# One PSUM pool of eight single banks, evictions by the bank, and a new list of jobs for all engines

## The chip, the cores and the metric

The kernel runs on one core of a Trainium2 chip. The metric is device time in microseconds (us). TensorE (PE) does the matrix products into PSUM, VectorE (DVE) and ScalarE (ACT) read PSUM and write SBUF, GpSimd (POOL) works from SBUF to SBUF, and SyncE (SP) issues the transfers. PSUM has eight banks; a bank holds 512 float32 values in each of 128 partitions.

## The reference

A retention layer (attention without softmax, with a decay by distance) feeds a gated MLP with spatial gating.

```python
# q, k, v: (8, 8, 576, 64) float32
scores = q @ k.T / sqrt(64)
Dmat   = where(i >= j, gamma[h] ** (i - j), 0)          # per head
x      = (scores * Dmat) @ v                            # heads side by side: (8, 576, 512)
h      = gelu_tanh(x @ w_in)                            # (8, 576, 1024)
u, v   = h[..., :512], h[..., 512:]
v_n    = (v - mean(v)) / sqrt(var(v) + 1e-6) * g_ln
v_s    = w_sg @ v_n + b_sg                              # over the sequence
out    = x + (u * v_s) @ w_out                          # (8, 576, 512) float32
```

## The kernel before, in words

The eight batches are taken as four pairs. A pair has 1152 rows, nine tiles (`m`) of 128 rows, and is cut into five blocks (`n`, table `RB`): four blocks of 256 rows and, in the middle, one of 128 rows that holds the end of the first batch and the start of the second. Block `b` is 5 times the pair plus `n`, so there are 20 blocks.

For each block:

- `a_load` fetches q, k and v (on SP). `a_prep` writes them to SBUF as bfloat16: q and v times powers of the decay, k as it is. POOL does nearly all of this; block 0 has its q on DVE and its k on ACT.
- `a_T` transposes q and k on PE, `a_Tev` copies the result out of PSUM (`qT`, `kT`). For blocks from 10 on, apart from the middle blocks, `a_TX` does it by DMA.
- `a_S(b, g)` makes the scores of chunks, `a_Sev` multiplies them by the causal mask into `ret`. `a_Z` makes the running state k.T @ v; `a_Zsum` and `a_Zev` add it up and turn it into bfloat16.
- `a_O` and `a_O2` make the output from `ret`, v, q and the state. `a_Oev` copies it to `xT`.
- `m_V` makes the gate half of x @ w_in, `m_Vg` is its gelu (ACT), `m_stats` the mean and variance (DVE), `m_rs` the reciprocal root (POOL), `m_norm` the normalization (ACT). `m_U` and `m_Ug` do the other half.

Once all tiles of a batch are normalized, `m_W` multiplies by `wT` (the transposed `w_sg`, made once by `build_wT` and `evac_wT`), `m_Wg` multiplies the gate into `uT` (DVE), `m_O` makes the output, `m_Oev` copies it out (ACT in the first pair, where PE adds x; DVE with `xr` in the others), and `m_store` stores it. At the start, `win_load`, `sg_load` and `wo_load` bring in the weights and cast them, on ACT with two casts on DVE (each job there is called `g`).

The order of all of this is written out by hand: every step is a job with a number, and `ORDER` lists the numbers. `emit` goes through the list and issues each job's instructions; each engine and the transfer queue of SP work in that order. In the list `f2w64` is a warm-up fill (matmuls of zeros), and `3@267` holds job 3 until PE is through with job 267.

PSUM is cut into two pools: `psP` with two slots of two banks for the transposed q and k, the scores and the attention outputs (all called `pp`), and `psD` with four single banks for the rest. Each pool hands out its slots in turn, in the order in which the jobs ask. The two banks of a `pp` slot are read by one instruction where DVE reads them (`a_Tev` L422, `a_Sev` L471), and by two, one for each bank, in `a_Oev` (L597).

Of the kernel before, what the change touches and what calls it, by code (L numbers as in the profile page):

```python
# [103 lines left out]
def kernel(  # L104
# [113 lines left out]
    def fill(spec):  # L218
# [3 lines left out]
        def f():  # L222
            scr = psD.tile([128, 512], F32, name="scr", tag="d")
            for _ in range(n):
                nc.tensor.matmul(scr[:, :w], warm[:, :128], warm[:, :w], start=True, stop=True, skip_group_check=True)
# [861 lines left out]
```

## Time and profile before

| | |
|---|---|
| time, median of 3 runs | 208.69 us (208.69 to 208.93) |
| span of the profiled execution, first to last instruction | 207.8 us |
| PE busy | 189.1 us, 91% |
| DVE busy | 146.6 us, 71% |
| ACT busy | 116.3 us, 56% |
| POOL busy | 118.3 us, 57% |
| moved by DMA | 50.45 MB, mean 243 GB/s |

The profile is of one execution. Its own time is not listed beside it; its span is 0.9 us below the median of the timed runs, which counts what lies ahead of the first and behind the last instruction too. Busy time of PE counts overlapping matmuls once, and a busy PE may still be at half its rate. In the groups of instructions, the number after "x" is the count, then come busy us and mean ns of one, then the engine's idle time before them and what ended it. In a row of the order in time come start, length, engine, line, and in square brackets the idle time before it.

### The profile page before, as it was taken

What the parts mean: (1) busy time and instruction counts of PE and PEld (TensorE: products, weight loads), DVE (VectorE), ACT (ScalarE), POOL (GpSimd) and SP (SyncE); (2) the same over time, 40 slices, a digit from 0 to 9 for tenths busy, and PEclk for the clock granted to TensorE, in tenths of its full rate; (3) what the DMA queues carried; (4) which work ended last, traced back from release to release, by engine and by line L of the source; (5) the groups of instructions that cost most, each with busy time, mean ns of one, the idle gap of its engine ahead of it and who ended that gap; (6) DMA issues with size and microseconds to landing.
All of it is one profiled execution on the core that took longest, in us unless ns stands there. A gap on an engine that the chain in (4) does not pass through costs nothing. (4 is left out here: it accounts for less than half of the span.)

```text
span 207.8 us, 7603 instructions
## 1 busy us (share of the span) xinstructions
PE 189.1 (91%) x3231; PEld 130.0 (63%) x3260; DVE 146.6 (71%) x287; ACT 116.3 (56%) x207; POOL 118.3 (57%) x169
## 2 busy tenths in 40 slices
PE   3277989999999979999999999999999999999992
PEld 3256467786667655666777676676675776556651
DVE  3767549897597669646968479669695648876672
ACT  5263398864659436689477565745827580536300
POOL 8747348864858799884659628760558813022000
PEclk9999999999999999999999999999999999999998
DMA  5999989989958999599999989999899999659765
GB/s 163 287 313 215 312 282 317 295 241 326 304 123 226 264 335 336 161 231 174 221 288 351 179 183 333 250 139 206 232 299 334 182 242 253 171 169 169 261 140 203
DMA packets 93844, 50.45 MB, mean 243 GB/s; under 512 B 44970, under 2 KB 87218, under 8 KB 93810
## 3 DMA queue, kind: packets, MB, share of 16 engines
q1 hardware_dynamic: 93792, 49.96, 93.8%
q8 instruction: 25, 0.41, 0.9%
q14 instruction: 9, 0.07, 0.1%
q10 hardware_dynamic: 18, 0.00, 0.0%
HBM read 32.79 MB, written 9.44 MB: 203 GB/s over the span
## 5 line engine op out<-in xcount | busy, mean ns | idle before, releaser
L471 DVE TENSOR_TENSOR ret<-pp,msk 128x1024 bf16<-128x1024 f32 x32 | 38.3, 1214 | 7.5 <-PE pp L458 7.4
L674 PE MATMUL wp<-wT,vn 128*128 128x288 bf16 x256 | 40.6, 286 | 0.0
L370 POOL TENSOR_TENSOR vb<-ld,gpow 128x1024 bf16<-128x1024 f32 (+1 forms) x20 | 34.5, 1731 | 10.2 <-PE pp L458 6.1
L608 PE MATMUL hv<-w_in,xT 128*128 128x512 bf16 x132 | 36.5, 393 | 1.9 <-ACT xT L597 1.0
L684 DVE TENSOR_TENSOR uT<-wp,uT 128x288 bf16<-128x288 f32 x64 | 27.6, 450 | 14.9 <-PE wp L674 10.3
L655 PE MATMUL hu<-xT,w_in 128*128 128x256 bf16 (+1 forms) x320 | 36.3, 262 | 0.0
L615 ACT ACTIVATE vg<-hv 128x512 f32<-128x512 f32 x36 | 21.2, 595 | 25.0 <-PE hv L608 20.7
L705 PE MATMUL op<-w_out,uT 128*128 128x512 bf16 (+1 forms) x131 | 33.5, 373 | 0.8 <-issue 0.2
L655 PEld LDWEIGHTS <-w_in 128*128 128x128 bf16 x320 | 28.1, 98 | 6.2
L623 DVE BATCH_NORM_STATS2 bst<-vg 128x6 f32<-128x512 f32 x36 | 24.6, 683 | 8.8 <-ACT vg L615 8.7
L597 ACT ACTIVATE xT<-pp 128x512 bf16<-128x512 f32 (+1 forms) x40 | 20.8, 549 | 17.2 <-PE pp L540 17.2
L370 POOL TENSOR_TENSOR qb<-ldq,gpow 128x1024 bf16<-128x1024 f32 x14 | 26.4, 1902 | 5.3 <-DMA ldq<-in_q_dram 5.3
L674 PEld LDWEIGHTS <-vn 128*128 128x128 bf16 x256 | 24.3, 98 | 8.2
L643 ACT ACTIVATE vn<-vg,mv 128x512 bf16<-128x512 f32 x32 | 25.2, 809 | 6.5 <-POOL mv L631 6.4
L628 POOL TENSOR_SCALAR mv<-mv 128x2 f32<-128x2 f32 (+1 forms) x20 | 4.5, 224 | 41.6 <-DVE mv L624 36.5
L665 ACT ACTIVATE uT<-hu 128x512 bf16<-128x512 f32 x36 | 20.7, 594 | 10.2 <-PE hu L655 10.1
L724 DVE TENSOR_TENSOR ob<-op,xr 128x512 f32<-128x512 f32 (+1 forms) x28 | 18.4, 669 | 5.8 <-PE op L705 5.5
L608 PEld LDWEIGHTS <-xT 128*128 128x128 bf16 x144 | 13.4, 100 | 14.2 <-ACT xT L597 1.6
L705 PEld LDWEIGHTS <-uT 128*128 128x128 bf16 x148 | 13.5, 98 | 11.4
L674 PE MATMUL wp<-wT,vmid 128*128 128x288 bf16 x64 | 18.2, 287 | 0.1
L360 POOL CAST kb<-ld 128x1024 bf16<-128x1024 f32 x14 | 14.5, 1037 | 4.8 <-DMA ld<-in_k_dram 4.8
L629 POOL TENSOR_TENSOR mv<-mv,mhalf 128x2 f32<-128x2 f32 (+1 forms) x20 | 14.1, 705 | 1.7
(100 smaller groups left out, 238.2 us busy)
## 6 DMA issues: line engine op xcount, KB each, us to landing
out_dram<-ob SPq DMA_DIRECT2D x35, 256.0 KB, 3.1
ld<-in_v_dram SPq DMA_DIRECT2D x16, 512.0 KB, 5.7
ld<-in_k_dram SPq DMA_DIRECT2D x16, 512.0 KB, 6.5
ldq<-in_q_dram SPq DMA_DIRECT2D x7, 1024.0 KB, 10.4
xT<-in_moe_w_sg_dram SPq DMA_DIRECT2D x2, 576.0 KB
ld<-in_q_dram SPq DMA_DIRECT2D x2, 512.0 KB, 5.2
xT<-in_moe_w_in_dram SPq DMA_DIRECT2D x1, 1024.0 KB
ld<-in_q_dram SPq DMA_DIRECT2D x8, 128.0 KB, 4.2
```

The source lines that it names most:

```text
L370: ve.tensor_tensor(dst, src, g.unsqueeze(len(src.shape) - 1).to_broadcast(list(src.shape)), op=Alu.mult)
L471: ins = nc.vector.tensor_tensor(ret[:].rearrange("p r (k t) -> p (r k) t", k=2), sc[:].rearrange("p r (k t) -> p (r k) t", k=2), (msk2 if ...
L597: nc.scalar.activation(dst, src, Act.Copy)
L608: ins = nc.tensor.matmul(hv[:], xTs[p][:, m, kk, :], w_in[:, kk, F2:], start=(kk == 0), stop=(kk == KK - 1))
L615: unfence(nc.scalar.activation(vgs[i][:], cur.pop(("hv", i))[:], Act.Gelu_apprx_tanh), ("V", i))
L623: nc.vector.bn_stats(bst[:], vgs[i][:])
L643: nc.scalar.activation(vn[:], vg[:], Act.Identity, scale=mv[:, s, 2:3], bias=mv[:, s, 3:4])
L655: ins = nc.tensor.matmul(hu[:, n, :], w_in[:, kk, 128 * c:128 * c + 128], xTs[p][:, m:m + w, kk, :], start=(kk == 0), stop=(kk == KK - 1), ...
L665: unfence(nc.scalar.activation(uTs[p][:, c0:c1, 128 * m:128 * m + 128 * w], cur.pop(("hu", i, half))[:], Act.Gelu_apprx_tanh), ("U", i, half))
L674: ins = nc.tensor.matmul(ps[:], vns[t0 + j][e][:, 128 * c:128 * c + 128], wT[e][j][:, half * HS:(half + 1) * HS], start=(j == 0), stop=(j ...
L684: ins = nc.vector.tensor_tensor(uTs[p][:, c, col:col + HS], cur.pop(("wp", b, c, half))[:], uTs[p][:, c, col:col + HS], op=Alu.mult)
L705: ins = nc.tensor.matmul(op[:], uTs[p][:, c, r], w_out[:, c, cs], start=(p >= XP and c == 0), stop=(c == KK - 1), skip_group_check=True)
```

## The change

- One pool `ps` of eight single banks takes the place of `psP` and `psD`. The tiles of two banks become two tiles of one bank each.
- `a_Tev` and `a_Sev` become two jobs each, one for each bank, so that there are 961 jobs in place of 913.
- A job may have an `alt`: another engine that can do it. In the list, `~` behind a number means that the job goes to that engine. A helper `copy` issues a copy on DVE, ACT or POOL; `m_norm` gets a DVE form (`tensor_scalar` with the scale and the bias), the casts of `w_out` too.
- Some dependencies become `after` or fall away, which matters only for whatever made the list, since the semaphores follow from the tiles.
- The list is new. It has one fill (`f4w192`, four products of 192 columns) in place of four (`f2w128`, `f2w64` twice, `f6w128`), and one hold (`876@857`) in place of eleven.

Jobs whose engine differs, by count:

| job | before | after |
|---|---|---|
| `a_Sev` | 36 DVE | 72 DVE (by the bank) |
| `a_Tev` | 12 DVE | 9 DVE, 15 ACT (by the bank) |
| `a_prep` | 58 POOL, 1 DVE, 1 ACT | 42 POOL, 11 DVE, 7 ACT |
| `m_norm` | 36 ACT | 19 ACT, 17 DVE |
| `a_Oev` | 40 ACT | 32 ACT, 8 DVE |
| `m_Oev` | 9 ACT, 28 DVE | 6 ACT, 31 DVE |
| `a_Zsum` | 32 DVE | 26 DVE, 6 ACT |
| `a_Zev` | 24 ACT | 19 ACT, 5 DVE |
| `evac_wT` | 10 DVE | 7 DVE, 3 ACT |
| weight casts `g` | 11 ACT, 2 DVE | 4 ACT, 9 DVE |

The diff, cut to its core (of the lists only their starts):

```diff
 ORDER = (
-    '0 2 103 73 105 1 f2w128 f2w64 7 17 6 75 76 8 77 78 108 109 104 267 22 269 72 3@267 106 107 268 270 12 13 195 81 '
...
+    '2 0 74 103~ 1 75 3 6 73 105~ 104 106 315 316~ 72 76 7 13 318 107~ 79 5~ 109~ 12 108~ 17 77 8 f4w192 4~ 207 210 '
+    '78 209 208 14 211 317 110 112 319~ 113 114~ 15 212 16 213 214 9 80 22~ 23 81 115 320 321 322 116 215 118 119 31 '
...
+            other, x = x[-1] == "~", x.rstrip("~")
...
-            j.fn()
+            j.fn(j.alt[0]) if other else j.fn()
...
-                xr=3, pp=2, d=4)
+                xr=3, d=8)
...
-    psP = ctx.enter_context(tc.tile_pool(name="psP", bufs=2, space=bass.MemoryType.PSUM))
-    psD = ctx.enter_context(tc.tile_pool(name="psD", bufs=4, space=bass.MemoryType.PSUM))
+    ps = ctx.enter_context(tc.tile_pool(name="ps", bufs=8, space=bass.MemoryType.PSUM))
+
+    def copy(eng, dst, src):
+        if eng == "ACT":
+            return nc.scalar.activation(dst, src, Act.Copy)
+        return (nc.vector if eng == "DVE" else nc.gpsimd).tensor_copy(dst, src)
...
+    def read(ins, what, n):
+        cur["left", what] = cur.get(("left", what), n) - 1
+        unfence(ins, what, cur["left", what] == 0)
...
-        tp = psP.tile([128, 2, 1024], BF, name="pp", tag="pp")
+        tp = [ps.tile([128, 1024], BF, name="tp", tag="d") for r in range(2)]
...
-    def a_Tev(b, t):
-        dst, w = new_T(b, t)
-        ins = nc.vector.tensor_copy(dst[:, :w].rearrange("p (c w) -> p c w", c=2), st.pop((b, "tp", t))[:, :, :w // 2])
-        unfence(ins, ("T", b, t))
+    def a_Tev(b, t, r, eng):
+        if ("Tw", b, t) not in cur:
+            cur["Tw", b, t] = new_T(b, t)
+        dst, w = cur["Tw", b, t]
+        ins = copy(eng, dst[:, r * w // 2:(r + 1) * w // 2], st.pop((b, "tp", t, r))[:, :w // 2])
+        read(ins, ("T", b, t), 2)
...
-        sc = psP.tile([128, 2, 512], F32, name="pp", tag="pp")
+        sc = [ps.tile([128, 512], F32, name="sc", tag="d") for r in range(2)]
...
-    def a_Sev(b, g):
+    def a_Sev(b, g, r):
...
+            m = (msk2 if joint(b) else msk4)[:].rearrange("p a b t -> p (a b t)").unsqueeze(1).to_broadcast([128, 2, 256])
+            ins = nc.vector.tensor_tensor(ret.rearrange("p (k t) -> p k t", k=2), sc[:].rearrange("p (k t) -> p k t", k=2), m, op=Alu.mult)
...
-        ot = psP.tile([128, 2, 512], F32, name="pp", tag="pp")
+        ot = [ps.tile([128, 512], F32, name="ot", tag="d") for c in range(2)]
...
-        nc.scalar.activation(dst, src, Act.Copy)
+        copy(eng, dst, src)
...
-    def m_norm(i):
+    def m_norm(i, eng="ACT"):
+        def norm(dst, src, scale, bias):
+            if eng == "ACT":
+                nc.scalar.activation(dst, src, Act.Identity, scale=scale, bias=bias)
+            else:
+                nc.vector.tensor_scalar(dst, src, scale, bias, op0=Alu.mult, op1=Alu.add)
```

More of the change, by code (lines that the diff above doesn't have):

```diff
@@ L62, with __init__ @@
 class Job:
-    def __init__(self, eng, dur, due, fn, deps=(), new=None, uses=(), mode=None, nbytes=0, run=0, what="", behind=None, since=0.0, lag=0.0, ins=0, port=False, parts=1):
+    def __init__(self, eng, dur, due, fn, deps=(), new=None, uses=(), mode=None, nbytes=0, run=0, what="", behind=None, since=0.0, lag=0.0, ins=0, port=False, parts=1, alt=None, after=()):
+        self.alt, self.after = alt, [d for d in after if d is not None]
         self.what, self.behind, self.since, self.lag, self.ins, self.port, self.parts = what, behind, since, lag, ins, port, parts
@@ L222, in f @@
         def f():
-            scr = psD.tile([128, 512], F32, name="scr", tag="d")
+            scr = ps.tile([128, 512], F32, name="scr", tag="d")
             for _ in range(n):
@@ L284, in sg_load @@
         ld.append(add("SP", 450.0, 0.0, f_last, new=b1, nbytes=64 * S * 4, run=2304))
-        return ld, [add("ACT", 677.0, 0.0, lambda j=j: g(j), deps=[ld[j // 2]], uses=[bA if j < 4 else b1]) for j in range(SB)]
+        return ld, [add("ACT", 677.0, 0.0, lambda eng="ACT", j=j: g(j, eng), deps=[ld[j // 2]], uses=[bA if j < 4 else b1], alt=("DVE", 420.0)) for j in range(SB)]
     def wo_load():
@@ L484, in a_Z @@
         ns, cs = RB[b % NBK][0], ZC[b % NBK]
-        z = {c: psD.tile([128, 256], F32, name="zp", tag="d") for c in cs}
+        z = {c: ps.tile([128, 256], F32, name="zp", tag="d") for c in cs}
         for c in cs:
@@ L694, in m_O @@
         cs = slice(0, DM) if hf is None else slice(hf * DM // 2, (hf + 1) * DM // 2)
-        op = psD.tile([128, cs.stop - cs.start], F32, name="op", tag="d")
+        op = ps.tile([128, cs.stop - cs.start], F32, name="op", tag="d")
         cur["op", i, hf] = op
@@ L875 @@
         kfst = not jn and half_of(b) == 0
-        jk = add(eng, 855.0 * h + 183, t0 - 4000.0, lambda b=b, eng=eng: a_prep(b, "k", None, eng),
-                 deps=[J["ld", b, "k"]] + (jqs if jn and b else [J["k", b - 1]] if not jn and not kfst else []), behind=jqs[0] if jn else None,
+        jk = add(eng, 855.0 * h + 183, t0 - 4000.0, lambda eng=eng, b=b: a_prep(b, "k", None, eng), alt=("POOL" if eng == "ACT" else "ACT", 855.0 * h + 183),
+                 deps=[J["ld", b, "k"]], after=jqs if jn else [J["k", b - 1]] if not kfst else [],
                  new=B_qkb["k", U_] if kfst else None,
                  uses=[B_ld[b, "k"]] + ([B_qkb["q", U_]] if jn else [] if kfst else [B_qkb["k", U_]]))
-        jvv = add("POOL", 1715.0 * h + 190, t0 - 2000.0, lambda b=b: a_prep(b, "v"), deps=[J["ld", b, "v"]],
+        jvv = add("POOL", 1715.0 * h + 190, t0 - 2000.0, lambda eng="POOL", b=b: a_prep(b, "v", None, eng), alt=("DVE", 126.0 + 1100.0 * h), deps=[J["ld", b, "v"]],
                   new=B_vb[b], uses=[B_ld[b, "v"]])
@@ L929 @@
                 B_run[b, c] = Buf("run")
-            J["run", b, c] = add("DVE", 400.0, due, lambda b=b, c=c: a_Zsum(b, c), deps=[jz] + ([J[("run",) + was]] if was else []),
+            J["run", b, c] = add("DVE", 400.0, due, lambda eng="DVE", b=b, c=c: a_Zsum(b, c, eng), alt=("ACT", 400.0) if fst else None, deps=[jz] + ([J[("run",) + was]] if was else []),
                                      new=B_zb[b, c] if fin else B_run[b, c], uses=[zpb[c]] + ([B_run[was]] if was else []))
@@ L950 @@
             fst = n == 0 and c == 0
-            J["x", b, c] = add("ACT", 600.0 if ns == 2 else 385.0, jO.due + 700.0 + 100 * c, lambda b=b, c=c: a_Oev(b, c),
-                               deps=[jO] + ([J["x", p * NBK, 0]] if not fst else []), new=B_x if fst else None,
-                               uses=[otb] + ([] if fst else [B_x]))
+            J["x", b, c] = add("ACT", 600.0 if ns == 2 else 385.0, jO.due + 700.0 + 100 * c, lambda eng="ACT", b=b, c=c: a_Oev(b, c, eng), alt=("DVE", 640.0 if ns == 2 else 375.0),
+                               deps=[jO], after=[J["x", p * NBK, 0]] if not fst else [], new=B_x if fst else None,
+                               uses=[otb[c]] + ([] if fst else [B_x]))
         B_mv = Buf("mv")
@@ L1044 @@
                                        uses=[B_x, B_u], mode="F", ins=17)
-                            jOe = add("ACT", 597.0, due + 700.0, lambda a=a: m_Oev(*a), deps=[jOut], uses=[db, obb])
+                            jOe = add("ACT", 597.0, due + 700.0, lambda eng="ACT", a=a: m_Oev(*a, eng), alt=("DVE", 640.0), deps=[jOut], uses=[db, obb])
                         else:
```

136 lines of the change are left out of this document (68 added, 68 removed), and 65 rows, old and new, of the table ORDER.

## The prediction, made before the changed kernel was run

> **What bounds the kernel now.** I read the page first: the shares of the engines, the chain that ended last, then the busy time by stages, then PE's order of work in the first 30 us.
>
> ```profile
> span 207.8 us, 7603 instructions
> PE 189.1 (91%) x3231; PEld 130.0 (63%) x3260; DVE 146.6 (71%) x287; ACT 116.3 (56%) x207; POOL 118.3 (57%) x169
> PE 34%; issue 1%; DVE 0%; DVEq 0%
> 0.00:30.00 30.00, 19.40 (x379) 13.79 (x382) 17.90 (x48) 15.31 (x26) 18.25 (x43) 1.00 0.95 256
> 30.00:203.00 173.00, 168.88 (x2848) 115.71 (x2874) 127.44 (x237) 101.03 (x182) 100.07 (x127) 1.00 0.96 242
> 203.00:207.80 4.80, 0.78 (x8) 0.45 (x5) 1.30 (x3) 0.00 (x0) 0.00 (x0) 0.87 0.55 203
> 40.00:50.00 10.00, 9.38 (x259) 7.35 (x257) 8.66 (x14) 6.67 (x12) 5.39 (x5) 1.00 0.94 292
> 70.00:80.00 10.00, 8.41 (x210) 6.17 (x210) 6.02 (x14) 4.07 (x8) 8.99 (x9) 1.00 1.14 313
> 76.77 0.64 PE L407 MATMUL pp<-ident,qb 64*128 64x64 bf16 x32 [1.54 <-POOL qb L370]
> ```
>
> The reader is to see three stages (the columns of a stage are its length, then PE, PEld, DVE, ACT and POOL busy, the granted clock, the DMA share and GB/s). From 30 to 203 us PE is the bound: busy 168.88 of 173.00, 4.1 idle. The chain that ended last is PE work back to 130 us. Of those 4.1, 1.59 lie in 70 to 80 us and 0.62 in 40 to 50. The one long stop there is 1.54 us before a transposition, waiting for POOL's q preparation while POOL is busy 8.99 of 10. DVE is busy 127.44 of 173.00, or 74%. The end, 4.8 us, is the last copies and stores and has the same jobs in both lists. PE's matmuls are the same in both kernels except warm-up fills. So the change can only gain in the first 30 us and in the 4.1 us, and can only lose by new idle time of PE.
>
> The span is 207.8 and the median of the runs 208.69, so 0.9 us lie outside the span. I take differences from the span and apply them to 208.69.
>
> **The change, term by term. The first 30 us.**
>
> ```profile
> 8.63 1.06 ACT L358 ACTIVATE qb<-ld 128x1024 bf16<-128x1024 f32 x1 [3.20 <-DMA ld<-in_k_dram]
> 10.31 1.03 PE L407 MATMUL pp<-ident,qb 64*128 64x64 bf16 x32
> 12.67 0.64 PE L458 MATMUL pp<-qT 64*64 64x128 bf16 x16 [1.32 <-DVE qT L422]
> 16.96 0.32 PE L540 MATMUL pp<-ret,vb 64*64 64x128 bf16 x2
> 10.45 0.51 SPq L248 DMA_DIRECT2D xT<-in_moe_w_in_dram  x1
> 19.11 0.69 DVE L255 CAST w_in<-xT 128x1024 bf16<-128x1024 f32 x1 [0.81 <-DMA xT<-in_moe_w_in_dram]
> 20.71 0.61 PE L608 MATMUL hv<-w_in,xT 128*128 128x512 bf16 x1 [0.77 <-ACT xT L597]
> 23.64 1.89 PE L608 MATMUL hv<-w_in,xT 128*128 128x512 bf16 x4
> 32.69 1.89 PE L608 MATMUL hv<-w_in,xT 128*128 128x512 bf16 x8
> 27.77 1.60 PE L225 MATMUL scr<-warm 128*128 128x128 f32 x12
> 29.60 0.81 PE L608 MATMUL hv<-w_in,xT 128*128 128x512 bf16 x3 [0.23 <-ACT xT L597]
> GB/s 163 287 313 215 312 282 317 295 241 326 304 123 226 264 335 336 161 231 174 221 288 351 179 183 333 250 139 206 232 299 334 182 242 253 171 169 169 261 140 203
> L422 DVE COPY qT<-pp 128x1024 bf16<-128x1024 bf16 x4 | 2.7, 681 | 0.0
> L257 ACT ACTIVATE w_in<-xT 128x1024 bf16<-128x1024 f32 x1 | 1.1, 1057 | 4.3 <-DMA xT<-in_moe_w_in_dram 4.3
> L370 DVE TENSOR_TENSOR qb<-ld,gpow 128x1024 bf16<-128x1024 f32 x1 | 1.2, 1226 | 1.6 <-DMA ld<-in_q_dram 1.6
> ```
>
> Before: k of block 0 lands at 8.63, transposition 10.31, first scores 12.67, first O 16.96, first m_V 20.71; all attention of blocks 0 to 2 and both m_V of block 0 are through at 27.77. Then 12 fills, and real work goes on at 29.60.
>
> After, by hand from these rows. k is again the third large load: ACT prepares it by 9.7, transposition and Z until 11.3. ACT then has one Zsum (0.4) and both halves of the transposition (1057 ns each, the row of a copy as long), so S(0,0) starts near 13.9, 1.2 us later than now. The load of w_in's gate half loses its hold (`3@267`) and goes fourth. With q, k, v it makes 2.6 MB; the slices (5.2 us each) have brought 2.3 MB by 10.4 us, so it lands near 12, not 19.1; q of block 1 (0.5 MB more) near 13.9. On DVE the w_in cast and that q preparation stand ahead of the S evictions: 13.9 + 1.23 = 15.1. Then come a 0.4 copy, three half evictions (about 0.69), a Zev and a half transposition: the fourth S half is done near 19.5 and O(0) starts there, 2.5 us later than now. But T(1), S(1,0) lie before it, T(2), S(1,1) behind it: m_V(0) near 22.5, and the last O of block 2 ends near 27.6, equal to today's 27.77 within my error of some 2 us. What follows is not fills but seven wT transpositions, listed right there; their sources are cast by DVE and ACT until about 28.3. PE so runs on at 28.3 in place of 29.60: **-1.3 us**. Bounds: if w_in and q land 2 us later, DVE passes that on whole, +0.7; if PE runs m_V(0) and m_V(1) fast, 1.7 better, -3.0.
>
> The 1.7 is the row at 23.64 against that at 32.69: 4 matmuls took 1.89 us and 8 took the same later, so early ones run at half rate although the stage's granted clock reads 1.00. TensorE: Matmul & The Clock Gate in the Trainium skill, section "What's actually happening", says that PE leaves half rate after about 3.4 us of sustained work. By that rule m_V(0) at 22.5, 3.6 us behind the first work in the gapless stretch that I find from 18.9, would run fast, and the sum would be the -3.0. The fast rows here start only behind 25 us of stops and starts, which neither proves nor refutes it; I leave it to a rival.
>
> **The engines behind 30 us.** Durations (mean ns is the second number behind the bar):
>
> ```profile
> L471 DVE TENSOR_TENSOR ret<-pp,msk 128x1024 bf16<-128x1024 f32 x32 | 38.3, 1214 | 7.5 <-PE pp L458 7.4
> L724 DVE TENSOR_TENSOR ob<-op,xr 128x512 f32<-128x512 f32 x26 | 17.7, 688 | 5.8 <-PE op L705 5.5
> L422 DVE COPY qT<-pp 128x2048 bf16<-128x2048 bf16 x5 | 6.1, 1214 | 2.1 <-PE pp L407 2.1
> L422 DVE COPY kT<-pp 128x2048 bf16<-128x2048 bf16 x3 | 3.7, 1222 | 1.9 <-PE pp L407 1.9
> L643 ACT ACTIVATE vn<-vg,mv 128x512 bf16<-128x512 f32 x32 | 25.2, 809 | 6.5 <-POOL mv L631 6.4
> L370 POOL TENSOR_TENSOR qb<-ldq,gpow 128x1024 bf16<-128x1024 f32 x14 | 26.4, 1902 | 5.3 <-DMA ldq<-in_q_dram 5.3
> L360 POOL CAST kb<-ld 128x1024 bf16<-128x1024 f32 x14 | 14.5, 1037 | 4.8 <-DMA ld<-in_k_dram 4.8
> L597 ACT ACTIVATE xT<-pp 128x512 bf16<-128x512 f32 x32 | 18.0, 592 | 16.7 <-PE pp L540 16.7
> L519 DVE COPY run<-zp 128x256 f32<-128x256 f32 x8 | 3.3, 414 | 0.7 <-PE zp L494 0.7
> ```
>
> The new list, decoded job by job, gives the moves. DVE: 32 S evictions as two halves of about 688 (2 x 688 - 1214 = 0.16 each, the four small ones about the same), +5.8. Twelve T evictions (6.1 + 3.7 + 2.7 us) become 7 halves of 681 and 2 of about 420, the other 15 go to ACT: -6.9. Preparations 1 to 11, at 1226: +12.3. Normalizations 17, in 21 instructions; no row shows one on DVE, the ends are the w_in cast (0.69 for 1024, so about 0.42 for 512) and L724 (0.69); I take 0.42, the nearer kind, a copy from SBUF with no second tensor: +8.8, at most +14.5. Eight Oev +5.2, three m_Oev +2.1, five Zev +2.0, seven weight casts +2.9; six Zsum -2.5, three wT -1.3. Sum: 146.6 + 28.4 = **175 us**. POOL loses seven q parts, three v and six k: 7 x 1.90 + 3 x 1.90 + 5 x 1.04 + 0.6 = 24.8, to 93. ACT gains 13.1 of T halves, 5.8 of k, 2.3 and 2.0 of Zsum and wT, and loses 17.0 of norms, 4.5 of Oev, 8.6 of the rest: 109. About 20 of DVE's 175 lie in the head, so behind it some 155 of 174, 89% where it was 74%. DVE becomes a near second to PE.
>
> **PSUM.** The pools held 2 double and 4 single banks, the new one 8 single ones, handed out in order. With 4.1 us of PE idle, waiting for a bank can cost no more than that today; I give the pooling nothing beyond the next line. A late reader now holds up whatever asks eight banks on, of any kind: its price stands in the DVE term.
>
> **The 4.1 us.** The 1.54 stop goes: POOL is rid of 24.8 us, and of that q its first half is on DVE. What is late next there is the same q's DMA and DVE's half, both with the relief of about one preparation. Of the 0.62 in 40 to 50 I take most: together **-2.0**. The ends: 0 (DVE is late in place of POOL) and -3.0 (some 1.1 is left, single waits of 0.05 to 0.16).
>
> **DVE's density.** Summing row durations of the listed DVE jobs between points of the list, and taking off the 6% by which neighbours overlap (my sum of the old list is 156, the page has 146.6), the stretch of PE work from 30 to 60 us holds about 31 us of DVE for 30 of PE; the three stretches of 30 us that follow hold 27 to 29 each. PE cannot lead by more than eight banks. I take **+1.2**, ends 0 and +5 (below).
>
> Fewer fills and holds, and other DMA orders on SP: nothing on the path behind 30 us, since the fills stand ahead of a wait that remains and SP's loads come earlier. If that cover is gone, a late load shows up as POOL waiting for DMA, 5.3 us on q now, off the path.
>
> Sum: -1.3 - 2.0 + 1.2 = -2.1; 208.69 - 2.1 = **206.6 us**. Its own range is 205.2 to 208.2.
>
> **The rivals.** *Slower: DVE's new work from SBUF and POOL's block each other, and DVE becomes the bound.*
>
> ```profile
> 34.41 0.68 DVE L255 CAST w_in<-uT 128x1024 bf16<-128x1024 f32 x1
> 34.56 0.98 POOL L629 TENSOR_TENSOR mv<-mv,mhalf 128x1 f32<-128x1 f32 x1
> L629 POOL TENSOR_TENSOR mv<-mv,mhalf x20: 570/713/977, 28.7 to 190.6; 128x2 f32<-128x2 f32 x16, 128x1 f32<-128x1 f32 x4
> ```
>
> POOL's small power took 0.98 beside DVE's cast where its least is 0.57: 0.41 longer, near the 0.53 that the cast still ran. Today there are hardly any such meetings, since DVE reads PSUM nearly always. After, some 34 DVE instructions behind the head read only SBUF (9 preparations, 21 norms, 4 casts), with POOL at work 93 of 207, 45%, and about 0.8 us of its 1.90 or 1.04 left: 34 x 0.45 x 0.8 = 12 us more for DVE, 167 of 174. In the dense stretch, with POOL busier, about 3.4 are added to 31: PE loses 4.4 there in place of 1.2, and about 0.7 elsewhere: 206.6 + 3.2 + 0.7 = **210.5**. It decides from 2.1 us of extra PE idle on. Against it: these waits fall partly where DVE has slack. SBUF — State Buffer in the Trainium skill, section "SBUF: two separate sides", says that DVE in its two-port modes or with two SBUF inputs and POOL hold a shared port for a whole instruction and the other blocks fully; the row at 34.56 agrees with its 0.41, and this rival is that rule.
>
> *More gain:* PE runs fast by m_V(0) and DVE's backlog is absorbed: 208.69 - 3.0 - 2.0 = **203.7**. For it: PE busy 19.40 of the first 30 us with much at half rate. Against it: the DVE chain in the head.
>
> *No change:* the half evictions on ACT and the wait for w_in delay the head by the 0.7 and POOL's stop returns as DVE's, less what is won in the rest: about **208.5**.
>
> **How the numbers follow.** Forecast 0.44, slower by blocking 0.31, more gain 0.16, no change 0.09. A measurement tells about 0.2% (0.4 us). Faster is forecast and more gain, 0.60; same 0.09; slower 0.31. The range reaches to both rivals, a little past for their unknown sizes (the norm's 0.69, the head's 2 us): 202.7 to 211.8; 205.2 to 208.2 is the likeliest one's own.
>
> **What would show it.** PE's wt transpositions start near 28 with no fills before; first m_V near 22; PE idle behind it below 4 us, with no stop for q near 77; DVE busy about 175, POOL about 93 (much above 93 means blocking), S halves near 0.69, norms on DVE near 0.42. Wrong if DVE's TENSOR_TENSOR from SBUF or the norms take far longer than 1.23 and 0.42, if PE's waits name DVE by more than 3 us, or if O(0) starts past 21.

## The result, and the profile after

The changed kernel takes 221.98 us (median; 220.06 to 224.51 in four executions) where the kernel before takes 208.69 (208.0 to 208.93) beside it: a ratio of 1.061, 95% interval 1.053 to 1.068. It is slower by 13.3 us; 206.6 was forecast. (Medians below are over all executions; the ratios leave out the disturbed ones.) The experiments are called e1 to e18.

The page of the changed kernel, span and busy time:

```profile
span 219.1 us, 7611 instructions
PE 189.6 (87%) x3244; PEld 129.9 (59%) x3244; DVE 184.3 (84%) x365; ACT 110.9 (51%) x193; POOL 98.5 (45%) x153
```

The profiled execution took 220.79 us. PE is busy as long as before (189.6 for 189.1), part of it now at a lower rate, so the 11.3 us that the span grew are idle time of PE or time at half rate. DVE is 9 us above the forecast 175.

By stages (columns: length, then PE, PEld, DVE, ACT and POOL busy with their counts, granted clock, DMA share, GB/s). The kernel before:

```profile
30.00:40.00 10.00, 10.00 (x158) 7.75 (x157) 8.63 (x19) 8.90 (x15) 8.66 (x12) 1.00 1.12 308
50.00:60.00 10.00, 9.79 (x166) 6.25 (x169) 6.63 (x12) 6.04 (x12) 7.42 (x8) 1.00 0.98 259
60.00:120.00 60.00, 57.70 (x1164) 40.39 (x1159) 42.27 (x78) 38.84 (x74) 44.88 (x53) 1.00 0.98 245
120.00:200.00 80.00, 79.06 (x1117) 52.45 (x1130) 59.00 (x112) 40.58 (x72) 33.72 (x51) 1.00 0.95 227
```

The same stages of the changed kernel, with 40 to 50 us (before: PE 9.38, clock 1.00):

```profile
30.00:40.00 10.00, 8.93 (x142) 6.58 (x139) 9.45 (x18) 7.78 (x13) 5.98 (x11) 1.00 1.03 283
40.00:50.00 10.00, 6.57 (x97) 3.98 (x90) 8.83 (x13) 2.91 (x5) 9.83 (x8) 0.75 1.12 307
50.00:60.00 10.00, 9.51 (x236) 6.78 (x234) 8.38 (x18) 5.96 (x9) 0.30 (x1) 0.91 0.98 244
60.00:120.00 60.00, 54.50 (x1115) 37.85 (x1116) 56.11 (x100) 37.93 (x70) 34.93 (x46) 1.00 0.88 227
120.00:200.00 80.00, 78.61 (x1172) 52.51 (x1171) 71.00 (x143) 35.97 (x68) 31.74 (x52) 1.00 0.99 208
```

The loss can be read off by subtraction. PE is busy 1.07 us less in 30 to 40. In 40 to 60 it is busy 3.09 less (16.08 for 19.17), and what it does there runs at a clock of 0.75 and 0.91, worth at most another 2.5 + 0.9 us. In 60 to 120 it is busy 3.20 less, in 120 to 200 0.45 less. Together that is at most 11.2 us; some 1.2 us is won ahead of 30 us, and the rest lies behind 200 us. So more than half of it falls in the 20 us from 40 to 60. (What the lower clock costs by itself is the question of e7 below.)

PE's order of work in the changed kernel, at the end of the head and at the stop (columns: start, us, engine, line, what, count, and in brackets the idle time before and what ended it):

```profile
18.46 0.40 PE L552 MATMUL ot<-ret,vb 64*64 64x128 bf16 x2
22.45 1.89 PE L620 MATMUL hv<-w_in,xT 128*128 128x512 bf16 x4
24.91 1.04 PE L620 MATMUL hv<-w_in,xT 128*128 128x512 bf16 x4
28.35 2.27 PE L809 MATMUL wtp<-ident,wnat 128*128 128x128 bf16 x35
...
42.47 0.42 PE L691 MATMUL wp<-wT,vn 128*128 128x288 bf16 x2
45.75 0.66 PE L691 MATMUL wp<-wT,vn 128*128 128x288 bf16 x2 [2.86 <-DVE vn L650]
...
46.44 1.17 PE L691 MATMUL wp<-wT,vn 128*128 128x288 bf16 x4
...
76.78 0.30 PE L691 MATMUL wp<-wT,vn 128*128 128x288 bf16 x1 [0.78 <-DVE vn L650]
```

The first `m_W` starts, and its third product waits 2.86 us for normalizations on DVE. Behind the stop four products take 1.17 us; without a stop four take 0.65 (the run e7 below). That is near half rate; the clocks of 0.75 and 0.91 in the two stages lack 3.4 us of full rate, which is 6.8 us at half.

What DVE and POOL do there, first DVE's normalizations, then POOL's multiplications:

```profile
31.63 0.55 DVE L650 TENSOR_SCALAR vn<-vg,mv 128x512 bf16<-128x512 f32 x1 [0.42 <-POOL mv L643]
32.46 2.07 DVE L650 TENSOR_SCALAR vn<-vg,mv 128x512 bf16<-128x512 f32 x1
41.88 3.81 DVE L650 TENSOR_SCALAR vn<-vg,mv 128x512 bf16<-128x512 f32 x2
```

```profile
32.34 1.90 POOL L375 TENSOR_TENSOR qb<-ldq,gpow 128x1024 bf16<-128x1024 f32 x1 [0.75 <-PE hv L620]
41.47 3.94 POOL L375 TENSOR_TENSOR vb<-ld,gpow 128x1024 bf16<-128x1024 f32 x2
```

Read them in pairs. With POOL idle a normalization takes 0.55. The one from 32.46 runs beside a POOL instruction that ends at 34.24, and ends at 34.53. The two from 41.88 end at 45.69, beside two POOL instructions that end at 45.41. Each looks held until POOL's instruction is over; this is called the hold below. Over the whole kernel (mean ns is the second number behind the bar; the second view has min/median/max):

```profile
L650 DVE TENSOR_SCALAR vn<-vg,mv 128x512 bf16<-128x512 f32 x13 | 15.9, 1231 | 0.8 <-POOL mv L643 0.8
L375 DVE TENSOR_TENSOR qb<-ldq,gpow 128x1024 bf16<-128x1024 f32 x7 | 11.4, 1632 | 0.0
L375 DVE TENSOR_TENSOR vb<-ld,gpow 128x1024 bf16<-128x1024 f32 x3 | 5.0, 1663 | 1.5 <-DMA ld<-in_v_dram 1.5
L485 DVE TENSOR_TENSOR ret<-sc,msk 128x512 bf16<-128x512 f32 x64 | 41.3, 682 | 4.8 <-PE sc L471 4.7
```

```profile
L650 DVE TENSOR_SCALAR vn<-vg,mv x13: 537/1223/2120, 31.6 to 200.3; 128x512 bf16<-128x512 f32 x13
```

What reads PSUM (the halves of S) takes its 0.68. What reads and writes SBUF alone does not: the 13 large normalizations are 8.9 us over 0.54 each, seven q preparations 2.8 and three v preparations 1.3 us over 1.226 each: 13.0 us together. (The eight small normalizations of the middle tiles, least 0.506, are not in this sum.)

### The profile page after: what moved, and what is told of

It is laid out like the page before. It is cut to its first block, busy times and chain, and to the rows that moved or that the text cites. A ratio compares the mean times of both kernels' runs of the same rounds, so it can differ in the third digit from the quotient of the medians.

```text
span 219.1 us, 7611 instructions
## 1 busy us (share of the span) xinstructions
PE 189.6 (87%) x3244; PEld 129.9 (59%) x3244; DVE 184.3 (84%) x365; ACT 110.9 (51%) x193; POOL 98.5 (45%) x153
## 5 line engine op out<-in xcount | busy, mean ns | idle before, releaser
L691 PE MATMUL wp<-wT,vn 128*128 128x288 bf16 x256 | 43.0, 295 | 3.6 <-DVE vn L650 3.6
L485 DVE TENSOR_TENSOR ret<-sc,msk 128x512 bf16<-128x512 f32 x64 | 41.3, 682 | 4.8 <-PE sc L471 4.7
L672 PE MATMUL hu<-xT,w_in 128*128 128x256 bf16 (+1 forms) x320 | 37.1, 262 | 0.6 <-DVE wT L149 0.6
L722 PE MATMUL op<-w_out,uT 128*128 128x512 bf16 (+1 forms) x148 | 36.0, 374 | 0.5 <-DVE uT L701 0.5
L691 PEld LDWEIGHTS <-vn 128*128 128x128 bf16 x256 | 25.0, 100 | 14.2 <-DVE vn L650 4.3
L375 POOL TENSOR_TENSOR vb<-ld,gpow 128x1024 bf16<-128x1024 f32 (+1 forms) x17 | 30.7, 1810 | 0.8 <-DMA ld<-in_v_dram 0.8
L148 ACT ACTIVATE xT<-ot 128x512 bf16<-128x512 f32 (+1 forms) x32 | 16.9, 562 | 17.3 <-PE ot L552 17.3
L648 ACT ACTIVATE vn<-vg,mv 128x512 bf16<-128x512 f32 x19 | 15.3, 810 | 14.8 <-POOL mv L643 14.7
L650 DVE TENSOR_SCALAR vn<-vg,mv 128x512 bf16<-128x512 f32 x13 | 15.9, 1231 | 0.8 <-POOL mv L643 0.8
L552 PE MATMUL ot<-qT,zb 64*64 64x128 bf16 (+1 forms) x256 | 12.6, 228 | 1.8 <-DVE ret L485 0.9
```

What stands on the lines that cost most here:

```text
L375: ve.tensor_tensor(dst, src, g.unsqueeze(len(src.shape) - 1).to_broadcast(list(src.shape)), op=Alu.mult)
L485: ins = nc.vector.tensor_tensor(ret.rearrange("p (k t) -> p k t", k=2), sc[:].rearrange("p (k t) -> p k t", k=2), m, op=Alu.mult)
L552: nc.tensor.matmul(ot[bank][64 * c:64 * c + 64, j * cs:(j + 1) * cs], lhsT, rhs, start=(bank, c) not in begun, stop=True, skip_group_check ...
L672: ins = nc.tensor.matmul(hu[:, n, :], w_in[:, kk, 128 * c:128 * c + 128], xTs[p][:, m:m + w, kk, :], start=(kk == 0), stop=(kk == KK - 1), ...
L691: ins = nc.tensor.matmul(wp[:], vns[t0 + j][e][:, 128 * c:128 * c + 128], wT[e][j][:, half * HS:(half + 1) * HS], start=(j == 0), stop=(j ...
L722: ins = nc.tensor.matmul(op[:], uTs[p][:, c, r], w_out[:, c, cs], start=(p >= XP and c == 0), stop=(c == KK - 1), skip_group_check=True)
```

## The experiments

Theory at the outset: DVE's new SBUF work and POOL hold each other up, and PE waits for it. Rivals: DVE has too much work of any kind; the new list is at fault by its order, whichever engine does what; the single-bank pool or the halves cost something. The last is taken first.

### The pool and the halves: e6

The changed kernel's program with the old list, each pair of halves in the place of the whole and all engines as before:

```diff
-ORDER = ('2 0 74 103~ 1 75 3 ...')
+ORDER = (the old list, renumbered; a_Tev and a_Sev as two entries; no ~)
```

> The changed kernel's code (one pool of eight banks, evictions by the bank) with the old list, its jobs renumbered and the two halves of an eviction side by side on DVE; engines, fills and holds as before. If the pool or the halves are to blame: 213 us or more. If the new list or its choice of engines is: within 1.5 us of the kernel before, 207.5 to 210, with DVE near 153 us (about 6 us more for the halves) and PE without a stop of over 2 us behind 30 us.

Measured: 209.21 us (ten executions, 207.80 to 210.65), ratio 1.003, interval 0.999 to 1.007. The pool and the halves cost nothing that shows; all of the loss is in the list and its engines.

### DVE's new work, taken away: e1, e4, e2, e3

e1 takes the `~` from the 17 normalizations, which go back to ACT. e4 has them on ACT too and puts on DVE, in the place of each, a `bn_stats` of the same input whose result nobody uses (it shares the three `bst` buffers of the real ones). e2 leaves the normalizations on DVE and gives nine preparations behind the head back to POOL. e3 does both, and three casts of `w_out` go to ACT.

```diff
-... 335~ ... 336~ ... 371~ ... 357~ ... 356~ ...   (17 normalizations: e1, e3)
+... 335  ... 336  ... 371  ... 357  ... 356  ...
-... 121~ ... 134~ ... 151~ ...   (9 preparations: e2, e3)
+... 121  ... 134  ... 151  ...
-... 30~ ... 27~ ... 29~ ...      (3 casts: e3)
+... 30  ... 27  ... 29  ...
+            if eng != "ACT":      # e4
+                nc.vector.bn_stats(bst[:src.shape[0]], src)
+            nc.scalar.activation(dst, src, Act.Identity, scale=scale, bias=bias)
```

Expected of e1:

> The changed kernel with the 17 normalizations back on ACT, everything else as in the change. Three theories. Blocking (DVE's instructions from SBUF alone and POOL's exclude each other): DVE loses 15.9 + 5.9 us of norms, POOL's mean for v falls back from 1970 to about 1910 ns, the 2.86 us stop of PE at 45.75 and the half-rate stretch behind it go; 209 to 213 us. Density (DVE has too much work of any kind): the same 209 to 213, since 21.8 us of DVE work are gone. Pool or list (the eight banks in turn, or the list itself): PE still waits as much in other places; 217 us or more.

Expected of e4:

> Norms on ACT as in the run before, but DVE runs in each of the 21 places an instruction that takes as long and reads the same tile alone (bn_stats, 682 ns, no two-port mode; its result is not used). Blocking: within 1.5 us of the run without the stand-in, since bn_stats meets POOL without a wait. Density: near the changed kernel, 217 us or more, since DVE is as full as by the norms' undisturbed 540 ns. Pool or list: 217 or more in both.

Expected of e2:

> The changed kernel with the nine q and v preparations behind the head back on POOL, norms still on DVE. Blocking: DVE loses some 15 us, but POOL gains 17 us of work for the 21 norms to meet, so the norms stay at 1.2 us or get longer; 214 to 220 us. Density: DVE is 15 us emptier, 211 to 215. Pool or list: 217 or more.

Expected of e3:

> Norms on ACT, the nine preparations on POOL and the three w_out casts on ACT: behind the head DVE then has hardly an instruction that reads only SBUF, while the pool, the halves, the T copies on ACT and the list stay. Blocking and density: 205 to 209 us, with the head's 1.3 us kept and PE idle behind it near 4 us. Pool or list: 214 or more.

Measured, with 208.75 for the kernel before (208.69 beside the changed kernel):

| run | time, us | ratio, interval | DVE busy, us |
|---|---|---|---|
| changed kernel | 221.98 | 1.061, 1.053 to 1.068 | 184.3 |
| e1 | 216.75 | 1.040, 1.030 to 1.050 | 160.6 |
| e4 | 218.80 | 1.050, 1.041 to 1.059 | 174.2 |
| e2 | 215.43 | 1.034, 1.026 to 1.042 | 175.7 |
| e3 | 215.35 | 1.035, 1.026 to 1.042 | 148.1 |

Each edit gives 3 to 7 us, and both together no more than one. e1 lies between what blocking (209 to 213) and the list (217 or more) would give, e2 where blocking would put it, and e3 is 6 us or more above the 205 to 209 that blocking and density both named: it fell to the list. e4 is 2 us over e1, on the side of density, but it does not settle what load on DVE costs without the hold: their intervals overlap. In e2 the normalizations grew longer, since POOL had more to do:

```profile
L650 DVE TENSOR_SCALAR vn<-vg,mv 128x512 bf16<-128x512 f32 x13 | 20.5, 1584 | 0.8 <-POOL mv L643 0.6
```

and the first `m_W` still stops for as long as in the changed kernel:

```profile
46.15 0.66 PE L691 MATMUL wp<-wT,vn 128*128 128x288 bf16 x2 [2.86 <-DVE vn L650]
```

The kernel was 6.5 us faster all the same. So what e2 wins is DVE time given back, not a shorter hold of the normalizations, and that one stop is not the whole loss. And from about 176 us of DVE downwards these edits win nothing more: e3 has 28 us less than e2 and the same time. Something else sets that floor for the list with these engines. In e3's order of work on PE the stop is still there, with ACT's name on it:

```profile
42.82 0.64 PE L471 MATMUL sc<-qT,kT 64*64 64x128 bf16 x32 [1.70 <-ACT kT L148]
...
45.82 0.66 PE L691 MATMUL wp<-wT,vn 128*128 128x288 bf16 x2 [2.00 <-ACT vn L648]
```

### POOL's hold, by the length of its instructions: e10, e13, e15

The engines and the list stay those of the changed kernel. POOL's 128x1024 multiplications are made in pieces: e10 halves those for v (its edit skips q's, which have one dimension less), e13 halves v's and q's, e15 quarters them.

```diff
-        ve.tensor_tensor(dst, src, g.unsqueeze(...).to_broadcast(...), op=Alu.mult)
...
+        n = 2 if eng == "POOL" and math.prod(list(src.shape)[1:]) == 1024 else 1      # e13; e15: 4
...
+        w = src.shape[1] // n
+        for r in range(n):
+            ve.tensor_tensor(dst[:, r * w:(r + 1) * w], src[:, r * w:(r + 1) * w], g[:, r * w:(r + 1) * w], op=Alu.mult)
```

Expected of e10:

> The changed kernel with each 128x1024 multiplication of POOL for v and q made as two of 128x512, about 1.05 us each instead of 1.90, nothing else. Theory (a norm on DVE that runs beside a POOL instruction is held until that POOL instruction ends): the mean of the 128x512 norms falls from 1.23 us towards 0.85 to 1.0 us, the longest from 2.12 to about 1.3 us, the two norms at 41.9 us take under 3 us instead of 3.81, DVE's sum falls by 3 to 6 us, and the time falls by 0 to 4 us (218 to 222), since POOL's own sum grows by some 3 us. Rival (both engines run at a shared, lower rate while they overlap): the norms' mean stays at 1.15 to 1.3 us with a longest near 2.1, and the time stays at 221 to 225 us.

Expected of e13:

> The changed kernel with POOL's 128x1024 multiplications for v and also for q made as two of 128x512 each (the halving of v alone gave 215.37 us, DVE 180.0 us, two norms at 41.9 us 2.10 instead of 3.81, and the norm beside the undivided q at 32.6 us still 1.98). Theory (a norm or a preparation on DVE waits until the POOL instruction beside it has ended, so its length follows POOL's instruction): the norm at 32.6 us falls to 1.0 to 1.5 us, the mean of the 128x512 norms from 0.98 to 0.75 to 0.9 us, and the time falls by 0 to 3 us more (212.5 to 215.5). Rival (what v's halves gave came from the moved end of POOL's work, not from the hold on DVE): the norm at 32.6 stays near 2 us and the time at 215 or above.

Expected of e15:

> The changed kernel with POOL's multiplications for v and q in four pieces of 256 columns (two where the first dimension has two), in place of one of 1024; in halves the time was 214.07 us, the mean of the 128x512 norms 0.92 us, the two norms at 41.9 us about 2.1. Theory (a norm waits for the end of the POOL instruction beside it, and an unhindered one takes 0.54): the two norms at 41.9 fall to 1.3 to 1.8 us and the mean to 0.7 to 0.85; POOL's sum grows by 2 to 5 us, and the time is 212 to 215.5 us. Rival (the norm gets in only where POOL has no next instruction ready): the two norms take as long as POOL's run of pieces, over 3 us, and the time goes back towards 218 to 222 us.

Measured: e10 215.37 us (1.031, 1.020 to 1.042), e13 214.07 (1.023, 1.017 to 1.029), e15 213.07 (210.40, 212.53, 213.61 and 213.92; no interval). The same normalizations in the order of DVE's work, e10, e13 and e15 in turn:

```profile
32.58 1.98 DVE L656 TENSOR_SCALAR vn<-vg,mv 128x512 bf16<-128x512 f32 x1
41.91 2.10 DVE L656 TENSOR_SCALAR vn<-vg,mv 128x512 bf16<-128x512 f32 x2
```

```profile
32.56 0.98 DVE L655 TENSOR_SCALAR vn<-vg,mv 128x512 bf16<-128x512 f32 x1
```

```profile
32.36 0.68 DVE L655 TENSOR_SCALAR vn<-vg,mv 128x512 bf16<-128x512 f32 x1
40.43 1.30 DVE L655 TENSOR_SCALAR vn<-vg,mv 128x512 bf16<-128x512 f32 x2
```

and from e15 the group, POOL's pieces for q, and POOL's order of work beside the pair:

```profile
L655 DVE TENSOR_SCALAR vn<-vg,mv 128x512 bf16<-128x512 f32 x13 | 9.0, 698 | 0.7 <-POOL mv L648 0.6
L380 POOL TENSOR_TENSOR qb<-ldq,gpow 128x256 bf16<-128x256 f32 x28 | 17.6, 660 | 0.6 <-DMA ldq<-in_q_dram 0.6
```

```profile
40.02 5.03 POOL L380 TENSOR_TENSOR vb<-ld,gpow 128x256 bf16<-128x256 f32 x8
```

The normalization beside q takes 2.07, 0.98 and 0.68 us with q in one, two and four pieces, and 1.98 in e10, where only v was cut. The pair beside v takes 3.81, 2.10 and 1.30. Its length follows POOL's instruction. POOL ran its eight pieces from 40.02 to 45.05 without a gap and the pair was done by 41.73: it is held for an instruction at a time, not for as long as POOL has work. The Trainium skill, page SBUF — State Buffer, section "SBUF: two separate sides", calls the port that DVE and POOL share "an exclusive lock, not a bandwidth split"; these lengths agree with that. POOL's sum grew from 98.5 to 113.5 us in e15, more than expected, and the kernel is 8.9 us faster than the changed one; e10 fell below its 218 to 222, e13 and e15 came as forecast.

Engines and list are the same in all three, so what is won is put down to the hold. Where it is won can be read off, since PE makes the same products in the same order: the 72nd product of `m_U` starts at 64.7 us in the changed kernel and at 60.4 in e15, the 200th at 133.7 and 126.4, the last at 205.0 and 197.1. So about half of it is there by the end of the stretch with the long stop; 3 us more come in the next 70 us. And what is left over the kernel before, 3.5 us by the medians (209.60 in that set), bounds what the new list costs with the engines that it was made for.

### The same work on DVE in the old list: e8, e11, e14

The kernel before with the 17 normalizations on DVE (e8), with `bn_stats` in their place and the normalizations left on ACT (e11), and e8 with POOL's multiplications halved (e14).

```diff
     def m_norm(i):                                   # ACT
+        eng = "DVE" if i in (the 17 tiles) else "ACT"   # e8, e14; e11: bn_stats on DVE there
```

Expected of e8:

> The kernel before with the same 17 normalizations on DVE, its own list and pools. Blocking: the norms take over 0.9 us in the mean beside POOL's busy 118 us (0.54 alone), DVE grows by over 20 us and the time by 2 to 6. Without blocking: 0.54 us each, DVE 11 us more of 147, the time within 1 us of 208.7 since DVE was 74% busy.

Expected of e11:

> The kernel before, old list, norms on ACT as they were, and on DVE, in the place of the same 17 norms' instructions, a bn_stats of the same input (about 0.69 us each, some 14 us in all; its result is used by nobody): DVE has as much more to do as with the norms, but of a kind that the traces show at one length (682 ns) beside POOL's work. Theory (what cost 17 us when the 17 norms went to DVE in this list was POOL's hold on them, 1.04 us instead of 0.54 with the longest over 2, at the places where PE waits): 208.5 to 213 us. Rival (it was DVE's load or its order in this list, whatever the instruction): 218 to 226 us.

Expected of e14:

> The kernel before with the same 17 norms on DVE (225.56 us; the control with bn_stats in their place 214.94) and POOL's multiplications for v and q in halves. Theory (10.6 us of the 16.8 us that the norms cost there are POOL's hold on them, and it is as long as a POOL instruction): the two norms at 44 us fall from 4.15 to about 2.2 us, the mean from 1.04 to 0.7 to 0.85 us, and the time from 225.6 to 217 to 221 us. Rival (the loss is the load on DVE and the hold is beside the point): 224 to 227 us.

Measured: e8 225.56 us (1.083, 1.076 to 1.089), e11 214.94 (1.029, 1.020 to 1.039), e14 223.45 (1.061, 1.050 to 1.072). None came as forecast: e8 lost 17 us where 2 to 6 were expected, e11 lies between its theory (up to 213) and its rival (218 or more), and e14's median above the 217 to 221 of its theory and just under its rival. PE's longest wait for DVE in e8, e11 and e14, from the lists of waits (total, times, longest):

```profile
PE pp L458 <- DVE kT L422: 7.8, 1, 7.8
```

```profile
PE pp L458 <- DVE kT L422: 3.2, 1, 3.2
```

```profile
PE pp L463 <- DVE kT L427: 6.1, 1, 6.1
```

In e8's order of work on DVE the transposed k of block 3 is queued behind two normalizations; the third row is the same two in e14:

```profile
44.06 4.15 DVE L640 TENSOR_SCALAR vn<-vg,mv 128x512 bf16<-128x512 f32 x2 [0.64 <-POOL mv L631]
48.73 1.23 DVE L422 COPY kT<-pp 128x2048 bf16<-128x2048 bf16 x1
...
43.56 2.43 DVE L645 TENSOR_SCALAR vn<-vg,mv 128x512 bf16<-128x512 f32 x2 [0.64 <-POOL mv L636]
```

Against the kernel before of the same set (208.25, 209.66 and 209.21), 17 normalizations on an engine that was 71% busy cost 17.3 us, and as much work of another kind in their places 5.3. Halving POOL's instructions shortens the pair from 4.15 to 2.43 us (of 43.56 to 45.99), near the 2.2 expected, and lowers the time by 2.1 us by the medians, 4.6 by the ratios, where 4.6 to 8.6 were expected. So the hold is not all of what the normalizations cost here, and how much of the 17.3 is the hold's stays open. Something else in between is seen in the row at 44.06: a normalization makes DVE, which works in order, wait for POOL's factors (0.64), with all that is queued behind it, and the `bn_stats` does not wait for them. What that costs by itself was not measured.

### The half rate behind the stop: e7

```diff
-... 356~ 372 378 ...
+... 356~ f8w192 372 378 ...
```

The changed kernel with a warm-up fill ahead of the first `m_W`, in the time that PE waits anyway.

> The changed kernel with one more fill (some 2.6 us of matmuls of zeros) ahead of the first W, in the place where PE sits idle from 42.9 to 45.75. The fill brings nothing nearer. If half of what that stop costs is the clock that falls behind it (6.8 us at half rate): 217 to 219 us, about 3 us better, with no half-rate stretch between 45 and 52 us. If the clock does not matter: 220 to 222, or worse by the fill.

Measured: 220.1 us, 1.057 (1.049 to 1.065). The order of work on PE:

```profile
42.36 2.87 PE L233 MATMUL scr<-warm 128*128 128x192 f32 x16
...
46.02 0.65 PE L691 MATMUL wp<-wT,vn 128*128 128x288 bf16 x4
```

and e7's stages:

```profile
40.00:50.00 10.00, 9.26 (x190) 7.17 (x189) 9.82 (x15) 2.91 (x5) 9.84 (x8) 1.00 1.04 300
50.00:60.00 10.00, 7.55 (x182) 5.14 (x176) 7.83 (x17) 5.96 (x9) 0.42 (x2) 1.00 1.08 272
```

The half rate of 45 to 52 us goes, and the time hardly moves, as for a clock that does not matter: PE is busy 7.55 in place of 9.51 in 50 to 60. The half rate followed from the stop for DVE, and most of what it cost PE would otherwise have spent in waiting. That it runs on at full rate behind a filled gap agrees in kind with the Trainium skill, page TensorE: Matmul & The Clock Gate, section "What's actually happening", where idleness closes the clock's gate and sustained work opens it. The page names an idle window of about 3.4 us; here a stop of 2.86 was enough, and the row decides.

### The order of the list: e5, e12, e18

e5: the new list behind the last O of block 2 with all 70 `~` taken off. e12: e3, and block 3's halves of the transposed q and k exchange engines. e18: e12 with normalizations 3 and 2 moved ahead of three evictions of U on ACT.

```diff
-... 127~ ... 131~ ...                    (e12, on e3)
+... 127  ... 131  ...
-... 354 357 369 333 124 356 372 378 ...  (e18, on e12)
+... 357 356 354 369 333 124 372 378 ...
```

Expected of e5:

> The new list, but behind the last O of block 2 every job on the engine that it had before (70 marks taken away). If the engine choices (blocking, or copies that stand behind others on ACT) make the loss: 206 to 210 us, and the stop of PE near 42 us is gone. If the new order itself does: 213 or more, with PE idle for 2 us or more between 40 and 50 us whatever the engines, and the clock at half behind it.

Expected of e12:

> The run with norms on ACT, nine preparations on POOL and three casts of w_out on ACT (215.35 us), with one more change: both halves of block 3's q and k transpositions that the new list leaves to or puts on ACT by turns go with their list marks taken away, so that the halves change engine (ACT and DVE exchange one q half and one k half). Theory (the stop of PE at 42.8 and 45.8 us is the new list's: ACT comes to kT's half only behind two norms and a U, while DVE stands idle from 40.9 to 43.5): the 1.70 us wait on kT goes or halves, the vn wait of 2.00 us shrinks, the half clock from 44.9 to 51.7 us shortens to 3.4 us or goes, and lost time at the 60 us mark falls by 2 to 5 us, the time by 1 to 4 us (211.5 to 214.5). Rival (the stop is set by POOL's factors, which the order puts 1 us later, and the norms on ACT, whichever engine takes the halves): stop and half clock as before, 215 to 216 us.

Expected of e18:

> The run with no norms, late preparations or casts of w_out on DVE and block 3's transposed halves exchanged (214.19 us), with one move in the list: norms 3 and 2 stand ahead of three evictions of U on ACT, not between and behind them. Theory (the stop of 2.11 us at 43.2 us is there because the list puts those evictions, 1.7 us, ahead of the norms that the first W needs): the wait of W for vn falls to 0.3 to 1.0 us, lost time at the 60 us mark falls by 1 to 3 us, and the time to 211.5 to 213.5 us. Rival (the next wait takes its place: W runs earlier into the wait at 56.5 us, or S and O stop for DVE): the wait goes and the time stays at 213.5 to 215 us.

Measured: e5 217.9 us (1.036, 1.025 to 1.047), e12 214.19 (1.025, 1.018 to 1.033), e18 212.33 (ten executions; 1.012, 1.006 to 1.018). The order of work on PE, e12 and then e18:

```profile
45.32 0.42 PE L691 MATMUL wp<-wT,vn 128*128 128x288 bf16 x2 [2.11 <-ACT vn L648]
```

```profile
43.45 0.42 PE L690 MATMUL wp<-wT,vn 128*128 128x288 bf16 x2 [0.81 <-ACT vn L647]
```

With its engine marks off, the new order is still slower than the old one by 3.6%: the order costs that much with the old engines. (The stop of 2 us and the half clock that e5's second case named did not come: the longest wait for `vn` is 1.5 us, and the clock from 40 to 60 us is 1.00.) In e12 the 1.70 us wait for k is gone and the time falls by about 1, though the wait for `vn` does not shrink; two entries moved in e18 take that wait from 2.11 to 0.81 us and the time down by another 1.9 us, as expected. So the list asks PE for the first `m_W` before its inputs are there, with the normalizations on DVE beside whole POOL instructions and on ACT alike, and that is part of the floor. It is not a loss of the order by itself: with its own engines and POOL in quarters (e15) the same order waits 0.35 us at that place and comes to 213.07, below e5 and e12 and near e18.

### Which stretch of the order: e9, e16, e17

e9: the new list up to the last O of block 2, then all other jobs in the old order. e16: 250 entries of the old list (to about 58.9 us), then the rest in the new order, default engines. e17: the same with the new list's marks.

```diff
+ORDER = new[:94] + [x for x in old if x is not in new[:94]]              # e9
+ORDER = old[:250] + [x.rstrip("~") for x in new if x is not in old[:250]]  # e16; e17 keeps the ~
```

Expected of e9:

> The changed kernel's program with a spliced list: the new list word for word up to the last O of block 2 (94 entries, with its engine marks), and from there every remaining job in the order of the old list on its default engine; the old list's fills of the head are left out. Theory (the head's gain is real and what is lost is lost behind it, by the order from 28 us on and by DVE's new work): the wT transpositions start near 28.3 instead of 29.6 and the span is 1.0 to 1.3 us under the kernel before, so 207.0 to 207.8 us, with lost time of TensorE about 1.3 us less at every later mark than in the old list's run. Rival (a head that runs ahead only meets DVE, POOL or the loads later, so the head is worth nothing by itself): 208.3 to 209.5 us, with a stop of PE between 30 and 50 us that eats the 1.3 us. Rival (the pool of eight banks is what slows the kernel): above 212 us.

Expected of e16:

> The changed kernel's program with the old list for its first 250 entries (to about 58.9 us in the run with the old list) and behind them every remaining job in the order of the new list, all on their default engines. Theory (what the new order costs with default engines, 215 to 218 us against 209.2, is lost between 30 and 60 us, where W is listed ahead of norms that are not ready; behind 60 us the two orders are alike): 208.5 to 210.5 us. Rival (the new order is worse all along): 212 to 216 us.

Expected of e17:

> As the run with the old list to 58.9 us and the new order behind it, but with the new list's 47 engine marks behind 58.9 us kept (norms, preparations of q and v and others on DVE). Theory (POOL's hold on DVE costs time behind 60 us too, where the changed kernel loses 4.5 us more than the kernel before): 1.5 to 5 us over the run with default engines, so 210.5 to 214.5 us. Rival (all of the loss is made before 60 us and the rest only shows its echo): within 1 us of the run with default engines.

Measured: e9 212.06 us (1.016, 1.009 to 1.024), e16 215.87 (1.031, 1.024 to 1.038), e17 216.49 (1.035, 1.029 to 1.040). e9 misses its theory and is slower than either rival for the head: with the old order behind it, the new head wins nothing. (Its third case, above 212 for the pool, is ruled out by e6.) On PE, e9's waits begin at once, and at 36.09 it stops 1.55 us for POOL's q:

```profile
29.55 1.04 PE L619 MATMUL hv<-w_in,xT 128*128 128x512 bf16 x3 [0.75 <-ACT xT L147]
```

e16 refutes that the loss of the order with default engines lies only in 30 to 60 us. From 60 to 120 us, e6 (old list) and then e16:

```profile
60.00:120.00 60.00, 59.39 (x1135) 40.92 (x1134) 43.95 (x98) 40.33 (x76) 44.88 (x53) 1.00 1.01 249
```

```profile
60.00:120.00 60.00, 53.42 (x1161) 37.09 (x1160) 41.34 (x90) 36.85 (x69) 44.45 (x50) 1.00 1.04 251
```

PE loses 6.0 us there. e17 lies within 1 us of e16, so the marks behind 58.9 us cost nothing that shows in this list. But each of the three lists is spliced from two, and a seam can lose time by itself, as e9 shows; they do not say how much the new order costs behind 60 us where it follows its own beginning. That stays open.

## Why the prediction was wrong

The step that failed is the price of DVE's new work, the +1.2 with its rival's 3.9, together with a list that was given no price of its own. Term by term:

*The head, -1.3.* The landmarks came as forecast: the `wT` transpositions at 28.35 (28.3), `m_V` at 22.45 (22.5), O(0) at 18.46 (19.5). The first `m_V` still ran at half rate (1.89), the second did not (1.04); the bound of -3.0 had both fast. But the old head is not fixed at 29.60: e16 and e17 have the same first 250 entries, and work behind the fills begins at 29.59 in one and 28.11 in the other. PE's order of work, e16 and then e17:

```profile
23.86 1.89 PE L619 MATMUL hv<-w_in,xT 128*128 128x512 bf16 x4
...
29.59 1.04 PE L619 MATMUL hv<-w_in,xT 128*128 128x512 bf16 x4
```

```profile
22.67 1.04 PE L620 MATMUL hv<-w_in,xT 128*128 128x512 bf16 x4
...
28.11 1.03 PE L620 MATMUL hv<-w_in,xT 128*128 128x512 bf16 x4
```

The second `m_V` takes 1.89 us in the one and 1.04 in the other; in e6, with these entries too, both take 1.04 and work goes on at 28.20. Whether PE is at full rate there changes from one execution to the next, by as much as the forecast gain; that a head came out within 0.1 us of the forecast is in part luck. Whether the kernel as a whole keeps any of it no run shows; e9 speaks against it.

*PSUM, 0.* Right (e6).

*DVE's rows.* Halves of S 0.69 (measured 0.682), `tensor_tensor` from SBUF 1226 where POOL leaves it alone: right. Normalizations 0.42: wrong, 0.54 undisturbed, and 1.23 as they fell.

*The 4.1 us, -2.0.* This step failed. The 1.54 us stop for POOL at 76.77 has gone, and at 76.78 PE stops 0.78 us for DVE's normalization instead (the row above); between 40 and 60, where 0.62 was to be won, over 6 us are lost. The bound of 0, "DVE is late in place of POOL", was a bound in name only, since it let DVE be just as late, not later.

*DVE's density, +1.2.* This is the step that decided. The rival had its mechanism, the hold, and nearly its size on DVE: 12 us forecast, 13 in the three groups above. It failed in the price: of the 12 us it let PE lose 3.9, on the ground that DVE has slack elsewhere. In the runs, cutting the hold short alone is worth up to 8.9 us (e15). About half of that is won around the first `m_W`, for which a held normalization comes late and ahead of which PE has nothing else listed; the other half is spread over what follows. I had priced the delay by averages over long stretches, DVE's sum against PE's; the place of the instruction in its queue decides what it costs, and the list says which ones PE waits for.

*Not in the sum at all.* A loss by the new order. With other engines than its own it is large: by the ratios 7.5 us over the kernel before with the old engines (e5), some 5.3 with DVE relieved of nearly all its new SBUF work (e12), 2.5 after one move (e18). With its own engines it is at most the 3.5 us that e15 leaves. I priced the engines of the new list and the head, and never went through its list behind the head to see whether PE's entries find their inputs ready; that the sequence of PE's work was "the same matmuls" stood for "no loss".

The parts do not add up to 13.3 us exactly, and cannot: they hide behind each other. From 221.98, the hold accounts for up to 8.9 (e15), other edits of DVE's work reach 6.6 (e2, e3), and e18, with nearly no hold and a short stop, comes to 212.33. Two different ways, a short hold in e15 and other engines with one move in e18, so end within 1 us of each other. No version with the new list is faster than the kernel before. What makes up the last 2.5 us (1.2%) is open.

## What to carry to other kernels

Price work that is moved to another engine by the consumer behind it: look in the queue for what stands behind the moved instruction and for who waits for that, not at the engine's busy share. Before moving an SBUF-to-SBUF instruction to DVE, look what POOL does at that time; if it must go there, cut POOL's instructions into pieces, since the hold is as long as one of them. An order fits one set of engines and durations: this one lost 8.9 us by held instructions and several us with other engines. So read a new order entry by entry at the places where a stage first needs another's result.
